# TensorE reads a run-time tile's second weights where they stand, by a register that holds the expert

## The chip, the cores and the metric

One core of one Trainium2 chip runs the whole program. The metric is the time of one execution on the device, in microseconds (us). The engines are named as in the profile: PE is TensorE (PEld its weight loads), DVE is VectorE, ACT is ScalarE, POOL is GpSimd and SP is SyncE. A `q` behind a name (PEldq, DVEq, SPq) marks an instruction that the engine's sequencer carries out itself.

## The reference

The first part is a gated recurrence along 4 sequences of 5056 steps with 256 channels. The second part is a layer of 8 experts: each of the 20224 tokens goes to the one expert with the largest gate logit.

```python
f = lower_bound + (1 - lower_bound) * sigmoid(f_logit)
for t in range(S):
    h = f[:, t] * h + (1 - f[:, t]) * x[:, t];  y[:, t] = h      # y: 20224 tokens x 256
logits = y @ w_gate;  e_idx = argmax(logits)                     # 8 experts
gate_w = softmax(logits)[e_idx];  eom = sigmoid(y @ w_output_gate)
for e in range(8):
    mask = e_idx == e
    h = max(y[mask] @ w1[e], 0)                                  # 256 -> 1024
    out[mask] = gate_w[mask] * eom[mask, e] * (h @ w2[e])        # 1024 -> 256
```

## The kernel before

Every float32 matrix product is made of three f16 products: both operands are split into a high and a low f16 half (hh and hl for the hidden layer, the index 0 and 1 in the weights), and high by high, high by low and low by high are added in PSUM.

**Work.** The tokens pass in 40 chunks of 512 (`chunk`, lines 254 to 439). A chunk is loaded, scanned (DVE, L280), split into halves (ACT L310, DVE L314), transposed to rows by SP's DMA (L307), multiplied with the gates on PE (L329), counted by expert on PE (L386), and its rows are scattered by POOL into a scratch memory in DRAM, sorted by expert (L433). At the same time the weights of all experts are scaled and split into `w1s` and `w2s`, which then stay in SBUF for good: `w2s` has for each expert 8 slices, each with a high and a low part of 256 columns.

**Tiles.** Once enough tokens of an expert have come, a plan (`plan`, L476 to L556) on DVE writes a table `pl_tab` with one row a tile: the place of its tokens and its expert. Which expert a tile has is known only at run time. A full tile has two blocks of 128 tokens (nb = 2); after the last chunk what is left of each expert is taken in tiles of one block (nb = 1). In the traced run 82 such run-time tiles were worked, 64 full ones and 18 of one block. Ahead of them, in the first 185 us, come tiles whose expert is fixed in the program (`first1`, `first2`), which read `w1s` and `w2s` where they stand; they are not touched here.

**A run-time tile.** `gather` fetches its tokens by SP's DMA. `expert` (L640) makes DVE's sequencer read the expert from the table into a register. `fetch1` (L654) and `fetch2` (L660) have DVE copy the expert's halves of `w1s` and `w2s`, 128x2048 f16 each, two of either a tile, into the fixed buffers `w1_0`, `w1_1`, `w2_0`, `w2_1`, of which there is one each. `gemm1` (L666) multiplies tokens with the first weights, 12 matmuls for each of four quarters q, ACT makes hh from PSUM (L680) and DVE makes hl (`low`, L688). `gemm2` (L693) multiplies hh and hl, which are loaded as stationary operands, with the second weights, which stream: 6 matmuls of 256 columns for each block and quarter, 48 for a full tile and 24 for one of one block. ACT scales the result (`evacuate`), POOL scatters it (`put`).

**Order.** `experts` (L925 to L963) writes the order by hand: in iteration t, quarter q, PE gets `gemm1` of tile t and then `gemm2` of tile t - 1. The DVE tasks of the quarter (`low`, `fetch1`, `fetch2`, `factors`) are mixed with those of the chunks in flight by `together`, and each engine keeps the order that results (`ordered`). `beside` puts the chunks' small matmuls (L329, L386) one at a time behind groups of three matmuls of `gemm1` and `gemm2`. `fetch2(T, 0)` stands in quarter 3 of tile T's own iteration and `fetch2(U, 1)` in quarter 1 of the next one, always ahead of the `gemm2` that needs it.

Of the kernel before, what the change touches and what calls it, by code (L numbers as in the profile page):

```python
# [9 lines left out]
F16 = mybir.dt.float16  # L10
# [6 lines left out]
ds = bass.ds  # L17
# [4 lines left out]
SMALL, BIG = 1, 2  # L22
# [28 lines left out]
def tile_scan_moe(  # L51
# [10 lines left out]
    nc = tc.nc  # L62
    P = 128
    D, N = xT.shape
    KD = D // P
    E = wgT.shape[2] // 2
    WE = wT.shape[2]
    NF = WE // (2 * D)
# [9 lines left out]
    WH = WE // 2  # L78
    QH = WH // 2
# [4 lines left out]
    def sure(tokens):  # L84
# [19 lines left out]
        out=tri, in_=ones, compare_op=ALU.is_gt, fill=0.0, base=0, pattern=[[1, P]], channel_multiplier=-1  # L104
# [63 lines left out]
    def alone(g):  # L168

        while True:  # L170
            try:
                next(g)
            except StopIteration as end:
                return end.value
# [6 lines left out]
        out=gsq, in0=wgf, scalar=1.0, in1=wgf, op0=ALU.mult, op1=ALU.mult, accum_out=gss  # L181
# [9 lines left out]
        out=wgs[:, :, 1, :], in0=wgc, scalar=gsc, in1=wgs[:, :, 0, :], op0=ALU.mult, op1=ALU.subtract  # L191
# [13 lines left out]
    w2f = w2s.rearrange("p e f h m -> p (e f h m)")  # L205
# [26 lines left out]
    def beside(n=None):  # L232
        for _ in range(len(queue) if n is None else min(n, len(queue))):
            f, a = queue.pop(0)
            f(*a)
# [386 lines left out]
    mpool = {}  # L622
# [17 lines left out]
    def expert(T):  # L640
        yield BIG
        T["ev"] = nc.vector.value_load(T["tab"][T["j"] : T["j"] + 1, 1:2], min_val=0, max_val=E - 1)

    def factors(T):
        nb, ev = T["nb"], T["ev"]
        col = cinv[:, ev : ev + 1] if isinstance(ev, int) else cinv[:, ds(ev, 1)]
        fac = sp.tile([P, 2], F32, tag="fac", name="fac", bufs=4)
        yield SMALL
        nc.vector.tensor_scalar(
            fac[:, 0:nb].unsqueeze(2), T["mt"][:, 0:nb, 0:2].bitcast(F32), col, None, ALU.mult  # L650
        )
        T["fac"] = fac

    def fetch1(T, h):  # L654
        w = mpool["m"].tile([P, QH * 2], F16, tag=f"w1_{h}", name=f"w1_{h}", bufs=1)
        yield BIG
        nc.vector.tensor_copy(out=w, in_=w1f[:, ds(T["ev"] * (2 * WH) + h * 2 * QH, 2 * QH)])  # L657
        T[f"w1_{h}"] = w.rearrange("p (f k h m) -> p f k h m", f=NF // 2, k=KD, h=2)

    def fetch2(T, h):  # L660
        w = mpool["m"].tile([P, QH * 2], F16, tag=f"w2_{h}", name=f"w2_{h}", bufs=1)
        yield BIG
        nc.vector.tensor_copy(out=w, in_=w2f[:, ds(T["ev"] * (2 * WH) + h * 2 * QH, 2 * QH)])  # L663
        T[f"w2_{h}"] = w.rearrange("p (f h m) -> p f h m", f=NF // 2, h=2)

    def gemm1(T, q):  # L666
        mp, n = mpool["m"], T["nb"] * P
        ph = pp.tile([P, 2, 256], F32, tag="h", name="ph", bufs=4)
        w = T[f"w1_{q // 2}"]
        for i in range(2):  # L670
            f = (2 * q + i) % 4
            for k in range(KD):
                first, last = k == 0, k == KD - 1
                o = ph[:, i, 0:n]
                nc.tensor.matmul(out=o, lhsT=w[:, f, k, 0, :], rhs=T["xh"][:, k, 0:n], start=first, stop=False)  # L675
                nc.tensor.matmul(out=o, lhsT=w[:, f, k, 0, :], rhs=T["xl"][:, k, 0:n], start=False, stop=False)  # L676
                nc.tensor.matmul(out=o, lhsT=w[:, f, k, 1, :], rhs=T["xh"][:, k, 0:n], start=False, stop=last)  # L677
                beside(1)
        hh = mp.tile([P, 2, 256], F16, tag="hh", name="hh", bufs=6)
        nc.scalar.activation(hh[:, :, 0:n], ph[:, :, 0:n], AF.Relu)  # L680
        T[f"h{q}"] = (ph, hh)

    def low(T, q):
        n = T["nb"] * P
        ph, hh = T[f"h{q}"]
        hl = mpool["m"].tile([P, 2, 256], F16, tag="hl", name="hl", bufs=6)
        yield BIG
        nc.vector.scalar_tensor_tensor(  # L688
            out=hl[:, :, 0:n], in0=ph[:, :, 0:n], scalar=0.0, in1=hh[:, :, 0:n], op0=ALU.max, op1=ALU.subtract
        )  # L690
        T[f"h{q}"] = (hh, hl)

    def gemm2(T, q):  # L693
        nb = T["nb"]
        if q == 0:
            T["y"] = pp.tile([P, 2, D], F32, tag="y", name="py", bufs=2)
        y, w = T["y"], T[f"w2_{q // 2}"]
        hh, hl = T.pop(f"h{q}")
        for i in range(2):
            f = (2 * q + i) % 4  # L700
            for b in range(nb):
                first = q == 0 and i == 0 and b == 0
                last = q == 3 and i == 1
                c = slice(b * P, (b + 1) * P)
                o = y[:, b, :]
                nc.tensor.matmul(out=o, lhsT=hh[:, i, c], rhs=w[:, f, 0, :], start=first, stop=False, skip_group_check=True)  # L706
                nc.tensor.matmul(out=o, lhsT=hh[:, i, c], rhs=w[:, f, 1, :], start=False, stop=False, skip_group_check=True)  # L707
                nc.tensor.matmul(out=o, lhsT=hl[:, i, c], rhs=w[:, f, 0, :], start=False, stop=last, skip_group_check=True)  # L708
                beside(1)


# [31 lines left out]
    def evacuate(T):  # L743
        nb = T["nb"]
        if isinstance(T["ev"], int):
            T["yo"] = yo = ep.tile([P, 1, D], F32, tag="ey", name="ey", bufs=2)
        else:
            T["yo"] = yo = mpool["m"].tile([P, 2, D], F32, tag="yo", name="yo", bufs=2)
        for b in range(nb):
            nc.scalar.activation(yo[:, b, :], T["y"][:, b, :], AF.Copy, scale=T["fac"][:, b : b + 1])  # L750

    def put(T):
        for b in range(T["nb"]):
            ins = nc.gpsimd.indirect_dma_start(  # L754
                out=out[:, :], out_offset=IOA(ap=T["mt"][:, b, 2:4].bitcast(I32), axis=0), in_=T["yo"][:, b, :],
                in_offset=None, bounds_check=N - 1, oob_is_err=False,
            )
            apart(ins, "out")
# [51 lines left out]
    def step(k, tasks, need=PLAN):  # L810
        prog["left"] += k
        if prog["left"] < 1.0:
            together(tasks)
        while prog["left"] >= 1.0:
            prog["left"] -= 1.0
            pump(tasks, need)
            tasks = []
# [3 lines left out]
    def ahead(t):  # L821
        while len(slots) <= t and len(slots) < ntile:
            plans(1)
            if planning:
                alone(planning.pop(0))
            else:
                pump([], 1)
        while prog["got"] <= t and prog["got"] < ntile:
            tiles[prog["got"]] = gather(prog["got"], slots[prog["got"]])
            prog["got"] += 1  # L830
# [52 lines left out]
    for j in range(-2, nh):  # L883
        tasks = []
# [4 lines left out]
        for z in range(2):  # L889
# [8 lines left out]
            tasks = []  # L898
# [26 lines left out]
    def experts(t0, t1, more):  # L925
        ahead(t0)
        alone(expert(tiles[t0]))
        alone(fetch1(tiles[t0], 0))
        for t in range(t0, t1 + 2):
            T = tiles.get(t) if t < t1 else None  # L930
            U = tiles.get(t - 1) if t0 < t <= t1 else None
            V = tiles.get(t - 2) if t > t0 + 1 else None
            rate = RATE * (T or U or V)["nb"] / 2
            for q in range(4):
                tasks = []
                if q == 0:
                    if t + 1 < t1 + min(more, 1):
                        ahead(t + 1)
                    if T:
                        tasks.append(fetch1(T, 1))  # L940
                elif q == 1:
                    if U:
                        tasks.append(fetch2(U, 1))
                elif q == 2:
                    if t + 1 < t1:
                        alone(expert(tiles[t + 1]))
                        tasks.append(fetch1(tiles[t + 1], 0))
                elif T:
                    tasks.append(fetch2(T, 0))
                    tasks.append(factors(T))  # L950
                if q == 0 and U:
                    tasks.append(low(U, 3))
                if q and T:
                    tasks.append(low(T, q - 1))
                step(rate, tasks)
                if q == 0 and V:
                    evacuate(V)
                if q == 1 and V:
                    put(V)
                if T:  # L960
                    gemm1(T, q)
                if U:
                    gemm2(U, q)  # L963
# [51 lines left out]
```

## Time and profile before

| | |
|---|---|
| time, median of 3 runs | 1020.92 us (1020.44 to 1021.68) |
| the profiled execution's own time | 1019.5 us |
| its span | 1017.8 us |
| PE busy | 917.6 us, 9775 matmuls |
| PEld busy | 822.5 us |
| DVE busy | 886.5 us, of which the copies of L663 111.9 us and of L657 114.9 us |
| ACT / POOL busy | 511.8 / 378.2 us |
| mean granted clock of TensorE | 0.989 |

Busy time is that of the engine alone, without its sequencer. The end of a matmul is modelled in the trace, so that matmuls that follow each other closely overlap in it: how fast PE runs is seen from the distance between the starts of matmuls, not from the length of one. L675 to L677 are `gemm1`'s matmuls, L706 to L708 `gemm2`'s.

### The profile page before, as it was taken

Reading aid. Unit: us, or ns where it says so; the run is one execution under the profiler, and the core shown is the slowest. Engines: PE = TensorE matmul, PEld = TensorE weight load, DVE = VectorE, ACT = ScalarE, POOL = GpSimd, SP = SyncE. Lnnn points to the kernel's source line nnn. Section 1 sums busy time; section 2 is a strip of 40 time slices with the busy share of each in tenths; the row PEclk is TensorE's granted clock in tenths of the full one; section 3 lists DMA queues with packets and bytes.
Section 4 is the critical chain, followed back from the end, with each engine's and each line's share of the span. In section 5 each row is a group of like instructions: output and inputs, shape, how many; then the busy total and the mean of one; then the engine's idle time right before and its main releaser. Section 6 shows DMA issues by size and latency. Waiting matters only on the chain. (4 is left out here: it accounts for less than half of the span.)

```text
span 1017.8 us, 27499 instructions
## 1 busy us (share of the span) xinstructions
PE 917.6 (90%) x9775; PEld 822.5 (81%) x9775; DVE 886.5 (87%) x2803; ACT 511.8 (50%) x1075; POOL 378.2 (37%) x378
## 2 busy tenths in 40 slices
PE   2267998899999999999999999999999999999993
PEld 2156987788888888888888888888888888899993
DVE  7889897899999999999999999999999998758771
ACT  5667684554554555545545455455455543333331
POOL 1532334334344443433444434344444344221121
PEclk9999999999999999999999999999999999999997
DMA  8899976755655556456566555565565644321120
GB/s 311 200 305 271 254 179 147 163 154 137 139 136 151 145 136 163 135 136 142 132 141 156 157 147 133 136 139 132 142 154 135 151 91 97 97 54 43 43 55 16
DMA packets 238546, 146.34 MB, mean 144 GB/s; under 512 B 202557, under 2 KB 204223, under 8 KB 238400
## 3 DMA queue, kind: packets, MB, share of 16 engines
q1 hardware_dynamic: 222752, 101.74, 43.5%
q0 software_dynamic: 15360, 42.74, 13.3%
q8 instruction: 80, 1.31, 0.6%
q14 instruction: 66, 0.54, 0.2%
q10 hardware_dynamic: 288, 0.02, 0.0%
HBM read 58.38 MB, written 44.49 MB: 101 GB/s over the span
## 5 line engine op out<-in xcount | busy, mean ns | idle before, releaser
L675 PE MATMUL ph<-xq,w 128*128 128x256 f16 (+1 forms) x1312 | 331.0, 261 | 3.2 <-DMA xq<-scr 2.7
L677 PE MATMUL ph<-xq,w 128*128 128x256 f16 (+1 forms) x1312 | 331.6, 261 | 0.0
L676 PE MATMUL ph<-xq,w 128*128 128x256 f16 (+1 forms) x1312 | 331.3, 261 | 0.0
L706 PE MATMUL py<-w,hh 128*128 128x256 f16 x1168 | 318.0, 272 | 10.4 <-DVE w L663 5.5
L708 PE MATMUL py<-w,hl 128*128 128x256 f16 x1168 | 318.3, 273 | 0.0
L707 PE MATMUL py<-w,hh 128*128 128x256 f16 x1168 | 318.2, 272 | 0.0
L754 POOL DMA_INDIRECT out_dram<-yo,mt x146 | 165.9, 1137 | 298.4 <-ACT yo L750 270.5
L433 POOL DMA_INDIRECT scr<-rows,dst x154 | 178.9, 1162 | 225.3 <-issue 212.5
L680 ACT ACTIVATE hh<-ph 128x512 f16<-128x512 f32 (+1 forms) x328 | 178.7, 545 | 156.9 <-PE ph L677 154.9
L688 DVE SCALAR_TENSOR_TENSOR hl<-ph,hh 128x512 f16<-128x512 f32 (+1 forms) x328 | 204.8, 625 | 10.4 <-ACT hh L680 8.6
L675 PEld LDWEIGHTS <-w 128*128 128x128 f16 x1312 | 128.0, 98 | 16.5 <-DVE xt L269 3.0
L677 PEld LDWEIGHTS <-w 128*128 128x128 f16 x1312 | 128.1, 98 | 12.1
L657 DVE COPY w<-w1s 128x2048 f16 x164 | 114.9, 701 | 26.2 <-PE ph L677 24.7
L676 PEld LDWEIGHTS <-w 128*128 128x128 f16 x1312 | 127.9, 97 | 9.7
L707 PEld LDWEIGHTS <-hh 128*128 128x128 f16 x1168 | 113.9, 98 | 23.2 <-issue 12.7
L708 PEld LDWEIGHTS <-hl 128*128 128x128 f16 x1168 | 113.9, 98 | 13.5
L706 PEld LDWEIGHTS <-hh 128*128 128x128 f16 x1168 | 113.9, 98 | 11.2
L663 DVE COPY w<-w2s 128x2048 f16 x164 | 111.9, 682 | 0.5 <-PE py L708 0.3
L274 ACT ACTIVATE ft<-ft,fb,fa 128x512 f32<-128x512 f32 (+1 forms) x76 | 60.6, 807 | 97.9 <-DVE xt L269 90.1
L310 ACT ACTIVATE ft<-xt,sa 128x512 f16<-128x512 f32 (+1 forms) x76 | 50.2, 708 | 104.9 <-DVE li L299 100.7
L280 DVE TENSOR_TENSOR_SCAN xt<-ft,xt 128x512 f32<-128x512 f32 (+4 forms) x78 | 90.9, 1173 | 0.0
L750 ACT ACTIVATE yo<-py,fac 128x256 f32<-128x256 f32 x146 | 61.5, 465 | 26.4 <-PE py L708 22.8
(172 smaller groups left out, 1355.0 us busy)
## 6 DMA issues: line engine op xcount, KB each, us to landing
ft<-in_fT_dram SPq DMA_DIRECT2D x37, 512.0 KB
xt<-in_xT_dram SPq DMA_DIRECT2D x37, 512.0 KB
w<-in_wT_dram SPq DMA_DIRECT2D x32, 512.0 KB
scr<-rows,dst POOLq DMA_INDIRECT x154, 2.8
rows<-ft SPq DMA_TRANSPOSE x152
out_dram<-yo,mt POOLq DMA_INDIRECT x146, 2.4
xq<-scr SPq DMA_TRANSPOSE x99
scr<-padt SPq DMA_DIRECT2D x9, 136.0 KB
```

Source lines behind the costliest of these rows:

```text
L433: ins = nc.gpsimd.indirect_dma_start(out=scr[:, :], out_offset=IOA(ap=dst[:, b : b + 1], axis=0), in_=rows[:, b, :], in_offset=None)
L657: nc.vector.tensor_copy(out=w, in_=w1f[:, ds(T["ev"] * (2 * WH) + h * 2 * QH, 2 * QH)])
L663: nc.vector.tensor_copy(out=w, in_=w2f[:, ds(T["ev"] * (2 * WH) + h * 2 * QH, 2 * QH)])
L675: nc.tensor.matmul(out=o, lhsT=w[:, f, k, 0, :], rhs=T["xh"][:, k, 0:n], start=first, stop=False)
L676: nc.tensor.matmul(out=o, lhsT=w[:, f, k, 0, :], rhs=T["xl"][:, k, 0:n], start=False, stop=False)
L677: nc.tensor.matmul(out=o, lhsT=w[:, f, k, 1, :], rhs=T["xh"][:, k, 0:n], start=False, stop=last)
L680: nc.scalar.activation(hh[:, :, 0:n], ph[:, :, 0:n], AF.Relu)
L688: nc.vector.scalar_tensor_tensor(out=hl[:, :, 0:n], in0=ph[:, :, 0:n], scalar=0.0, in1=hh[:, :, 0:n], op0=ALU.max, op1=ALU.subtract)
L706: nc.tensor.matmul(out=o, lhsT=hh[:, i, c], rhs=w[:, f, 0, :], start=first, stop=False, skip_group_check=True)
L707: nc.tensor.matmul(out=o, lhsT=hh[:, i, c], rhs=w[:, f, 1, :], start=False, stop=False, skip_group_check=True)
L708: nc.tensor.matmul(out=o, lhsT=hl[:, i, c], rhs=w[:, f, 0, :], start=False, stop=last, skip_group_check=True)
L754: ins = nc.gpsimd.indirect_dma_start(out=out[:, :], out_offset=IOA(ap=T["mt"][:, b, 2:4].bitcast(I32), axis=0), in_=T["yo"][:, b, :], in_o ...
```

## The change

`fetch2` is gone, and with it two DVE copies of 128x2048 for each run-time tile and the buffers `w2_0` and `w2_1`. Instead PE's own sequencer reads the tile's expert from `pl_tab` into a register, once a tile, at the head of `gemm2`'s first quarter (L691 of the changed kernel). Each of `gemm2`'s matmuls then takes its streaming operand straight out of `w2s`, at an address that is worked out from that register. `gemm1` and its copies (`fetch1`) stay as they were, as do the number, shapes and order of all matmuls.

```diff
-    def fetch2(T, h):
-        w = mpool["m"].tile([P, QH * 2], F16, tag=f"w2_{h}", name=f"w2_{h}", bufs=1)
-        yield BIG
-        nc.vector.tensor_copy(out=w, in_=w2f[:, ds(T["ev"] * (2 * WH) + h * 2 * QH, 2 * QH)])
-        T[f"w2_{h}"] = w.rearrange("p (f h m) -> p f h m", f=NF // 2, h=2)
-
     def gemm1(T, q):
...
         nb = T["nb"]
         if q == 0:
             T["y"] = pp.tile([P, 2, D], F32, tag="y", name="py", bufs=2)
-        y, w = T["y"], T[f"w2_{q // 2}"]
+            T["pv"] = nc.tensor.value_load(T["tab"][T["j"] : T["j"] + 1, 1:2], min_val=0, max_val=E - 1)
+        y = T["y"]
         hh, hl = T.pop(f"h{q}")
         for i in range(2):
-            f = (2 * q + i) % 4
+            at = T["pv"] * (2 * WH) + (2 * q + i) * (2 * D)
+            wh, wl = w2f[:, ds(at, D)], w2f[:, ds(at + D, D)]
             for b in range(nb):
...
-                nc.tensor.matmul(out=o, lhsT=hh[:, i, c], rhs=w[:, f, 0, :], start=first, stop=False, skip_group_check=True)
-                nc.tensor.matmul(out=o, lhsT=hh[:, i, c], rhs=w[:, f, 1, :], start=False, stop=False, skip_group_check=True)
-                nc.tensor.matmul(out=o, lhsT=hl[:, i, c], rhs=w[:, f, 0, :], start=False, stop=last, skip_group_check=True)
+                nc.tensor.matmul(out=o, lhsT=hh[:, i, c], rhs=wh, start=first, stop=False, skip_group_check=True)
+                nc.tensor.matmul(out=o, lhsT=hh[:, i, c], rhs=wl, start=False, stop=False, skip_group_check=True)
+                nc.tensor.matmul(out=o, lhsT=hl[:, i, c], rhs=wh, start=False, stop=last, skip_group_check=True)
...
-                elif q == 1:
-                    if U:
-                        tasks.append(fetch2(U, 1))
...
-                elif T:
-                    tasks.append(fetch2(T, 0))
+                elif q == 3 and T:
                     tasks.append(factors(T))
```

In the changed kernel `gemm1`'s matmuls stand on lines 669 to 671, `low` on 682 and `gemm2`'s matmuls on 702 to 704.

PE's instructions at the start of a full tile's `gemm2`, before the change. The three groups are the first block's high by high, high by low and low by high product; `w_0` is the copied buffer:

```order
L329 MATMUL pr<-wgs,ft 128x16
L706 LDWEIGHTS hh
L706 MATMUL py<-w_0_9416,hh 128x256
L707 LDWEIGHTS hh
L707 MATMUL py<-w_0_9416,hh 128x256
L708 LDWEIGHTS hl
L708 MATMUL py<-w_0_9416,hl 128x256
```

The same place in the changed kernel:

```order
L329 MATMUL pr<-wgs,ft 128x16
L691 TENSOR_LOAD pl_tab
L691 ISA x2
L702 LDWEIGHTS hh
L702 ISA
L702 MATMUL py<-w2s,hh 128x256
L703 LDWEIGHTS hh
L703 ISA
L703 MATMUL py<-w2s,hh 128x256
L704 LDWEIGHTS hl
L704 ISA
L704 MATMUL py<-w2s,hl 128x256
```

Three instructions for the sequencer stand ahead of the tile's first matmul (the load of the register and two that check its value), and one `ISA` stands between every weight load and its matmul: a fused group of three or four register operations, (expert x 4096 + place) x 2 + base, worked out anew for each matmul. The rest of PE's list, and the lists of ACT, POOL and SP, are the same in both kernels.

DVE's instructions in a quarter 2 and the quarters behind it, while a chunk is split into halves (L314), before the change. `w_0` and `w_1` are the buffers of the copies:

```order
L642 TENSOR_LOAD pl_tab
L642 ISA x2
L314 SCALAR_TENSOR_TENSOR ft<-xt,sa,ft 128x512
L657 ISA
L657 COPY w_0_8934<-w1s 128x2048
L688 SCALAR_TENSOR_TENSOR hl<-ph,hh 128x512
L314 SCALAR_TENSOR_TENSOR ft<-xt,sa,ft 128x512
L649 ISA
L649 TENSOR_SCALAR fac<-mt,cinv 128x2
L269 SCALAR_TENSOR_TENSOR xt<-ft,xt 128x512
L663 ISA
L663 COPY w_0_8969<-w2s 128x2048
```

The same place in the changed kernel:

```order
L642 TENSOR_LOAD pl_tab
L642 ISA x2
L314 SCALAR_TENSOR_TENSOR ft<-xt,sa,ft 128x512
L657 ISA
L657 COPY w_0_6310<-w1s 128x2048
L682 SCALAR_TENSOR_TENSOR hl<-ph,hh 128x512
L314 SCALAR_TENSOR_TENSOR ft<-xt,sa,ft 128x512
L649 ISA
L649 TENSOR_SCALAR fac<-mt,cinv 128x2
L269 SCALAR_TENSOR_TENSOR xt<-ft,xt 128x512
L682 SCALAR_TENSOR_TENSOR hl<-ph,hh 128x512
L269 SCALAR_TENSOR_TENSOR xt<-ft,xt 128x512
```

The copy out of `w2s` and its register operations are gone; what stood behind them has moved up. `fetch1`'s copies stay, as does DVE's own load of the expert (L642), which they need.

## The prediction

> **What bounds the kernel now.** I read the page first, then the table by stretches, then the rows of single lines, the waits of the middle stretch, and last the timeline of one chunk.
>
> ```profile
> PE 917.6 (90%) x9775; PEld 822.5 (81%) x9775; DVE 886.5 (87%) x2803; ACT 511.8 (50%) x1075; POOL 378.2 (37%) x378
> ```
>
> PE and DVE are both near full on average. The table by stretches (busy time and count of each engine, granted clock, DMA) parts the span at the first full tile, at the last chunk, and at the tiles of one block:
>
> ```profile
> core 0: us, PE busy (x) PEld busy (x) DVE busy (x) ACT busy (x) POOL busy (x), PEclk, DMA share, GB/s
> 0.00:185.00 185.00, 122.35 (x1652) 111.88 (x1652) 154.96 (x548) 119.18 (x216) 61.73 (x78) 0.98 0.89 234
> 204.00:835.00 631.00, 613.46 (x6025) 543.64 (x6023) 588.15 (x1880) 323.59 (x700) 267.54 (x252) 1.00 0.57 141
> 835.00:906.00 71.00, 71.00 (x683) 63.86 (x681) 53.75 (x177) 23.24 (x49) 21.35 (x21) 1.00 0.34 83
> 912.00:991.00 79.00, 79.00 (x1078) 74.97 (x1077) 62.73 (x136) 29.71 (x74) 16.20 (x15) 1.00 0.22 47
> ```
>
> From 835 us on PE never rests. In the middle stretch it is idle for 17.5 us and DVE is at 93%. The first stretch has no run-time tile, so the change cannot touch it. PE's sequencer has one wait a run-time tile just ahead of `gemm1`, which marks the tiles (last two numbers: start of the first and the last one), for the middle and for the tiles of one block:
>
> ```profile
> L675 PEldq EVENT_SEMAPHORE  x57: 51/51/51, 204.1 to 834.9; - x57
> ```
> ```profile
> L675 PEldq EVENT_SEMAPHORE  x16: 51/51/51, 912.0 to 991.5; - x16
> ```
>
> That is 630.8 / 56 = 11.26 us a full tile and 79.5 / 15 = 5.30 us a tile of one block. What the array itself needs is read from starts in PE's timeline (start, length, line):
>
> ```profile
> 505.48 0.27 PE L675 MATMUL ph<-xq,w 128*128 128x256 f16 x1
> ...
> 508.10 0.27 PE L675 MATMUL ph<-xq,w 128*128 128x256 f16 x1
> ...
> 508.42 0.20 PE L329 MATMUL pr<-wgs,ft 128*128 128x32 f16 x2
> 508.48 0.27 PE L675 MATMUL ph<-xq,w 128*128 128x256 f16 x1
> ```
>
> Between the first two starts lie 12 matmuls of `gemm1` and 12 of `gemm2`: 2.62 / 24 = 0.109 us each. Two gate matmuls take 0.06 us, 0.03 each with its load. A full tile needs 96 x 0.109 = 10.46 us, and half a chunk's 23 small matmuls (16 gates, 5 counts, 2 sums) 0.35: 10.81. So in the middle 0.45 us a tile, 25 us over 56 tiles, is waiting. Where:
>
> ```profile
> 508.80 0.17 PE L329 MATMUL pr<-wgs,ft 128*128 128x16 f16 x1
> 509.23 0.18 PE L329 MATMUL pr<-wgs,ft 128*128 128x16 f16 x1 [0.25 <-DVE ft L314]
> ...
> 509.97 0.20 PE L329 MATMUL pr<-wgs,ft 128*128 128x16 f16 x2
> 510.56 0.27 PE L706 MATMUL py<-w,hh 128*128 128x256 f16 x1 [0.39 <-issue]
> ```
> ```profile
> 508.42 0.75 DVE L314 SCALAR_TENSOR_TENSOR ft<-xt,sa,ft 128x512 f16<-128x512 f32 x1
> ...
> 509.82 0.68 DVE L663 COPY w<-w2s 128x2048 f16 x1
> ```
>
> Two stalls stand close together. At 508.80 PE is held for 0.43 - 0.03 = 0.40 us by DVE's L314. At 509.97 it is held for 0.59 - 0.06 = 0.53 us; the row says "issue", but the copy of L663 ends at 509.82 + 0.68 = 510.50, just ahead of the restart, so it is `fetch2` that PE waits for. The waits of the middle stretch count them:
>
> ```profile
> PE pr L329 <- DVE ft L314: 6.3, 26, 0.4
> PE py L706 <- DVE w L663: 5.5, 14, 0.4
> PE py L706 <- issue: 4.3, 11, 0.4
> ```
>
> About 26 of each, once a chunk: 26 x (0.40 + 0.53) = 24.2 us, nearly all of the 25. (The view gives less for each since the modelled end of a matmul lies 0.16 us behind the start of the next.) The kernel is bound by the array at 0.109 us a matmul, and by a DVE that is late once a chunk.
>
> **What the change removes.**
>
> ```profile
> L663 DVE COPY w<-w2s 128x2048 f16 x164 | 111.9, 682 | 0.5 <-PE py L708 0.3
> ```
>
> 164 copies of 0.68 us leave DVE. By itself that is worth nothing, since DVE is not what most of the time waits for; it is worth what PE waited. The 0.53 us stall was the wait for such a copy: it goes, 26 x 0.53 = 13.8 us. The one at L314 is lateness: DVE runs without a pause into it, four copies of a chunk are 4 x 0.6 = 2.4 us (it starts the next instruction 0.6 us behind a copy's start), and what is lacking is 0.40 us. It should go too, 26 x 0.40 = 10.4 us. Next late are the two chunk sums on PE, which wait for ACT; they are in the last us of the 25 and stay.
>
> **What it adds.** No engine work, but work for PE's sequencer: one register load a tile, and a group of register operations ahead of each matmul of `gemm2`. No trace of before shows either on PE. The nearest rows are DVE's, the same operations for the same addresses (min/median/max in ns):
>
> ```profile
> L642 DVEq TENSOR_LOAD <-pl_tab x82: 298/303/557, 183.6 to 988.8; - x82
> L642 DVEq FUSED_REGOPS  x82: 190/190/213, 184.3 to 989.2; - x82
> L642 DVEq SEQ_ASSERT  x82: 23/23/35, 184.5 to 989.5; - x82
> ```
> ```profile
> L663 DVEq FUSED_REGOPS  x164: 65/70/75, 192.6 to 998.1; - x164
> ...
> L663 DVEq EVENT_SEMAPHORE  x41: 21/21/21, 878.8 to 998.2; - x41
> ```
>
> The head of a tile costs 0.30 + 0.19 + 0.02, with 0.03 between each about 0.61 us. Behind it are queued only that tile's `gemm2` and what follows on PE; the table was written long before, since SP read it to fetch the tile. For one matmul, call the sequencer's whole time X. The group is 65 ns with three operations and 75 with four, and nearly all have four. PE's own simple wait takes 51 ns where DVE's takes 21, so I add 30. Load and matmul add 0.03, as for the gates. X = 75 + 30 + 30 = 0.135 us. Does a register in a matmul's address cost more? On DVE it does not show:
>
> ```profile
> L657 DVEq FUSED_REGOPS  x2: 65/70/75, 506.6 to 507.3; - x2
> ```
> ```profile
> L649 DVEq FUSED_REGOPS  x1: 53/53/53, 506.8 to 506.8; - x1
> ```
>
> Between these two, 506.6 to 506.8, DVE's sequencer did the group and handed over three instructions, one of them a copy with a register address: (200 - 65) / 3 = 45 ns for each at most. The bounds of X are 0.095 (65 + 30) and 0.25 (190, the longest group on any row here, + 60); I take 0.135, from the rows of the same operation.
>
> [...]
>
> X is longer than 0.109, so `gemm2` alone would starve the array. What hides it is `gemm1`, 12 plain matmuls that the sequencer hands over in 12 x 0.03 = 0.36 us while the array takes 1.31, and the distance that it runs ahead. In one tile:
>
> ```profile
> L675 PEldq EVENT_SEMAPHORE x1: 51/51/51, 495.5 to 495.5; - x1
> ```
> ```profile
> 497.49 0.27 PE L675 MATMUL ph<-xq,w 128*128 128x256 f16 x1
> ```
>
> The wait and the matmul right behind it in the list lie 1.9 us apart. A quarter's `gemm2` uses up 12 x (0.135 - 0.109) = 0.31 us of that, the head of a tile 0.61. The sequencer's sum for a full tile is 48 X + 48 x 0.03 + 0.35 + 0.05 + 0.61 = 48 X + 2.45: 8.9 us against the array's 10.81. It keeps up as long as X is under 0.174; if that cover is gone, each 0.01 us of X costs 0.48 us a tile. In a tile of one block `gemm1` has 48 matmuls of 128 columns and `gemm2` 24: the sequencer needs 24 X + 2.1 = 5.34 us against 5.30, 0.04 x 18 = 0.7 us, so about 1.
>
> [...]
>
> **Sum.** -13.8 - 10.4 + 1 = -23.2, of which I leave 1.2 for stalls that don't go wholly: -22. Against the profiled execution, 1019.5 us (span 1017.8): 997.5. The median of the runs is 1.4 us above that execution: 999.
>
> **The rivals.** [...]
>
> Second, about the same: the copy's stall goes, the other stays because L314 is held by what comes before it (ACT's halves and SP's transposes) and not by copies, and X is 0.165. Then -13.8, and in the tiles of one block 6.06 - 5.30 = 0.76 x 18 = +14: 1021. Against it: DVE's 93%.
>
> **How the numbers follow.** The forecast has 0.60: from 994 (nothing is left of the 25 us and the head is hidden) to 1011 (X = 0.165, -24 + 14). The slower rival has 0.30, half of it below 1100. The second has 0.10, mostly within 0.2% (2 us, about what a measurement of this kernel can tell from no change). Faster 0.63, same 0.07, slower 0.30. The range goes from 993 to 1100; what lies above has about 0.15, below it 0.03.
>
> **What would show it.** In the profile of the changed kernel: DVE's busy time down by about 112 us; no wait of `gemm2`'s first line (L702); the register groups' row on PE, with its length; waits of L669 in the middle 10.85 us apart instead of 11.26, and 5.3 in the tiles of one block. I am wrong if these lie 12 and 6.9 us apart, with matmuls of `gemm2` that start 0.2 us apart and no releaser; and half right if L329 still waits for L314.

## The result and the profile after

| | before | after |
|---|---|---|
| time, median | 1020.68 us (1020.25 to 1021.68, 4 runs) | 990.01 us (988.36 to 993.38, 4 runs) |
| the profiled execution, its span | 1019.5, 1017.8 us | 990.77, 989.1 us |

The ratio is 0.9702, with a 95% interval of 0.9675 to 0.973: 3% faster. The forecast of 999 had the direction right and was 9 us too high; 990.0 lies 3 us below the range.

The page of the changed kernel, engines:

```profile
span 989.1 us, 30907 instructions
PE 907.7 (92%) x9775; PEld 819.7 (83%) x9775; DVE 801.0 (81%) x2639; ACT 519.7 (53%) x1075; POOL 390.1 (39%) x378
```

DVE has 164 instructions fewer (2639 instead of 2803). Its busy time fell by 886.5 - 801.0 = 85.5 us, not by the 111.9 us that the copies' own lengths add up to: in the record a copy of 0.68 us overlaps what follows it, which starts 0.60 us behind the copy's start (median), and with each copy 85.5 / 164 = 0.52 us of busy time went away. The table by stretches, for the middle and for the tiles of one block:

```profile
core 0: us, PE busy (x) PEld busy (x) DVE busy (x) ACT busy (x) POOL busy (x), PEclk, DMA share, GB/s
204.00:810.00 606.00, 606.00 (x6052) 543.52 (x6051) 536.85 (x1783) 332.90 (x706) 283.66 (x253) 1.00 0.61 147
882.00:962.00 80.00, 80.00 (x1091) 75.92 (x1089) 45.92 (x107) 30.17 (x76) 15.41 (x16) 1.00 0.23 50
```

PE never rests in the middle any more, and DVE is at 89% instead of 93%. The waits that mark the tiles (L669 is what L675 was), for the middle and for the tiles of one block:

```profile
L669 PEldq EVENT_SEMAPHORE  x57: 51/51/51, 203.6 to 806.8; - x57
```
```profile
L669 PEldq EVENT_SEMAPHORE  x16: 51/51/51, 883.6 to 963.1; - x16
```

A full tile takes 603.2 / 56 = 10.77 us instead of 11.26, and a tile of one block 79.5 / 15 = 5.30 us as before. So the 28.7 us between the two profiled executions' spans lie almost all in one place: (11.264 - 10.771) x 56 = 27.6 us in the middle, 0.5 us ahead of it (204.1 against 203.6), and 0.6 us behind it (1017.8 - 834.9 = 182.9 against 989.1 - 806.8 = 182.3).

The view of waits has no row at all for PE between 196 and 970 us. Who waits now, from the same view over all engines:

```profile
ACT hh L674 <- PE ph L671: 297.4, 257, 2.1
...
DVE hl L682 <- ACT hh L674: 55.4, 91, 2.1
DVE w L657 <- PE ph L671: 33.3, 65, 1.3
...
DVE ft L314 <- ACT ft L265: 18.3, 27, 1.0
```

DVE and ACT wait for PE (first number: us in all, then how often). In the kernel before, PE had waits of its own there, which the prediction shows: 26 for L314 and 25 at L706. Also in the middle, ACT waited for DVE's scans (L280), and DVE for a transfer:

```profile
ACT ft L287 <- DVE xt L280: 36.9, 28, 1.5
...
DVE ft L314 <- DMA rows<-ft: 12.8, 20, 0.6
```

Both rows are gone in the changed kernel. The second shows that of the 7% of the middle in which DVE was not busy (631 - 588 = 43 us), 12.8 us were put down to the transposes at L314. DVE's pause at L314 itself has stayed: the last row of the view of after has it once a chunk, put down to ACT.

What was added, on PE's sequencer: the groups of register operations ahead of `gemm2`'s matmuls, and the head of a tile (min/median/max in ns).

```profile
L702 PEldq FUSED_REGOPS  x1168: 51/55/60, 193.8 to 972.1; - x195
```
```profile
L691 PEldq TENSOR_LOAD <-pl_tab x82: 297/301/637, 192.8 to 968.4; - x82
L691 PEldq FUSED_REGOPS  x82: 151/151/165, 193.5 to 968.8; - x82
L691 PEldq SEQ_ASSERT  x82: 18/18/24, 193.7 to 969.0; - x82
```

For one tile's head, the load (the second of the two, at 963.6) and the first group behind it:

```profile
L691 PEldq TENSOR_LOAD <-pl_tab x2: 303/304/306, 958.3 to 963.6; - x2
```
```profile
L702 PEldq FUSED_REGOPS  x1: 51/51/51, 964.3 to 964.3; - x1
```

That is 0.70 us for a head.

### The profile page after: what moved, and what is told of

It is laid out like the page before. It is cut to its first block, busy times and chain, and to the rows that moved or that the text cites. A ratio compares the mean times of both kernels' runs of the same rounds, so it can differ in the third digit from the quotient of the medians.

```text
span 989.1 us, 30907 instructions
## 1 busy us (share of the span) xinstructions
PE 907.7 (92%) x9775; PEld 819.7 (83%) x9775; DVE 801.0 (81%) x2639; ACT 519.7 (53%) x1075; POOL 390.1 (39%) x378
## 5 line engine op out<-in xcount | busy, mean ns | idle before, releaser
L669 PE MATMUL ph<-xq,w 128*128 128x256 f16 (+1 forms) x1312 | 330.4, 260 | 2.9 <-DMA xq<-scr 2.4
L750 POOL DMA_INDIRECT out_dram<-yo,mt x146 | 175.3, 1201 | 363.2 <-ACT yo L746 339.9
L704 PE MATMUL py<-w2s,hl 128*128 x1168 | 318.5, 273 | 0.0
L703 PE MATMUL py<-w2s,hh 128*128 x1168 | 318.4, 273 | 0.0
L702 PE MATMUL py<-w2s,hh 128*128 x1168 | 318.1, 272 | 0.0
L433 POOL DMA_INDIRECT scr<-rows,dst x154 | 175.7, 1141 | 122.6 <-issue 109.3
L657 DVE COPY w<-w1s 128x2048 f16 x164 | 120.3, 734 | 35.1 <-PE ph L671 33.3
L669 PEld LDWEIGHTS <-w 128*128 128x128 f16 x1312 | 127.9, 98 | 14.3 <-DVE fac L649 2.7
L704 PEld LDWEIGHTS <-hl 128*128 128x128 f16 x1168 | 114.1, 98 | 13.8
L280 DVE TENSOR_TENSOR_SCAN xt<-ft,xt 128x512 f32<-128x512 f32 (+4 forms) x78 | 90.8, 1172 | 0.0
L314 DVE SCALAR_TENSOR_TENSOR ft<-xt,sa,ft 128x512 f16<-128x512 f32 (+1 forms) x76 | 56.2, 744 | 20.1 <-ACT ft L265 18.3
L329 PEld LDWEIGHTS <-ft 128*128 128x128 f16 x600 | 51.7, 99 | 15.1 <-ACT ft L310 4.9
```

Of the source, the lines that this page charges most:

```text
L280: nc.vector.tensor_tensor_scan(out=xt[:, k, a:z], data0=ft[:, k, a:z], data1=xt[:, k, a:z], initial=init, op0=ALU.mult, op1=ALU.add)
L433: ins = nc.gpsimd.indirect_dma_start(out=scr[:, :], out_offset=IOA(ap=dst[:, b : b + 1], axis=0), in_=rows[:, b, :], in_offset=None)
L702: nc.tensor.matmul(out=o, lhsT=hh[:, i, c], rhs=wh, start=first, stop=False, skip_group_check=True)
L703: nc.tensor.matmul(out=o, lhsT=hh[:, i, c], rhs=wl, start=False, stop=False, skip_group_check=True)
L704: nc.tensor.matmul(out=o, lhsT=hl[:, i, c], rhs=wh, start=False, stop=last, skip_group_check=True)
L750: ins = nc.gpsimd.indirect_dma_start(out=out[:, :], out_offset=IOA(ap=T["mt"][:, b, 2:4].bitcast(I32), axis=0), in_=T["yo"][:, b, :], in_o ...
```

## The experiments

Two theories could explain the gain. **Two places**: PE waited once a chunk at each of two places, for a copy and for L314, and each wait belongs to what stands there (the prediction's sum). **Load**: DVE as a whole needed longer for a chunk (two full tiles, 22.5 us, its own pauses included) than PE (21.54 us), and PE paid the difference at whatever it took from DVE last. The rivals on PE's sequencer were tested as well: that its new work costs time, or would with a little more of it.

The three groups of four runs were made on three chips. On the first the kernel before took 1018.8 us (median), on the second 1029.0, on the third 1028.7; ratios are to the kernel before in the same group.

### Both copies back, read by nobody

The changed kernel, with DVE still copying both halves at the old places:

```diff
+    def idle2(T, h):
+        w = mpool["m"].tile([P, QH * 2], F16, tag=f"w2_{h}", name=f"w2_{h}", bufs=1)
+        yield BIG
+        nc.vector.tensor_copy(out=w, in_=w2f[:, ds(T["ev"] * (2 * WH) + h * 2 * QH, 2 * QH)])
...
+                elif q == 1:
+                    if U:
+                        tasks.append(idle2(U, 1))
...
                 elif q == 3 and T:
+                    tasks.append(idle2(T, 0))
                     tasks.append(factors(T))
```

> The changed kernel with both copies of a tile's second weights put back on DVE, at their old places, into buffers that nobody reads; PE still reads w2s by the register. Theory of load (DVE as a whole sets the pace of the middle stage: in the kernel before it worked without a pause at about 22.5 us a chunk, PE needs 21.5): the pace of before comes back though PE waits for no copy, about 1019 us (1014 to 1021), with PE waiting at other lines for DVE. Theory of two places (0.53 us lost at the copy, 0.40 at L314, as predicted): only L314's stall and that of the chunk sums come back, 990 + 13 = about 1003 us. If only the wait for the copied buffer counted: 990 us.

Measured: 1018.31 us, ratio 0.9982 (0.9967 to 0.9998). The whole gain is gone, although no matmul waits for these copies. Tiles in the middle, and PE's waits there:

```profile
L674 PEldq EVENT_SEMAPHORE  x54: 51/51/51, 205.1 to 801.7; - x54
```
```profile
PE pv L291 <- ACT ft L287: 6.2, 21, 0.4
PE pr L329 <- DVE ft L314: 5.5, 24, 0.4
```

And ACT's wait for DVE's scan there, which the changed kernel doesn't have:

```profile
ACT ft L287 <- DVE xt L280: 35.9, 26, 1.5
```

596.6 / 53 = 11.26 us a tile, as before. PE still stands twice a chunk: the wait that was at the copy's reader has moved to the chunk sum L291, which waits for ACT, which waits for DVE. That rules out two places and is what load says. What PE's own new work costs is not seen here, since PE has slack while DVE sets the pace (it is busy for 583.5 us of the 596 between 204 and 800 us); it is seen in the changed kernel, whose array is dense at 10.77 us a tile with all of that work, and in two kernels below, which both take 988 us, one with all of that work (one copy back) and one with half of it (one half by register).

### One copy back, read by nobody

The same with only the copy of the first half (`idle2(T, 0)` in quarter 3).

> The changed kernel with one of the two copies of a tile put back on DVE (the one of quarter 3), unread. Load: DVE then needs 22.5 - 2 x 0.6 = 21.3 us a chunk, less than PE's 21.5, so the time stays at 990 us (988 to 994). Two places: L314 is late again by part of its 0.40 us, 990 to 997 us.

Measured: 988.07 us, ratio 0.9696 (0.9674 to 0.9718): no different from the changed kernel. One copy a tile costs nothing and the next one everything.

```profile
204.00:810.00 606.00, 606.00 (x6053) 543.57 (x6051) 560.02 (x1841) 331.63 (x704) 284.18 (x254) 1.00 0.60 147
```

In this row of the table by stretches DVE is busy for 560.0 us of 606, nearly as long as in the kernel before (564.8 us in the same stretch), and PE is dense all the same. DVE's busy share alone doesn't tell which side of the edge a kernel is on.

### The copies asked for a quarter earlier

The kernel before, with `fetch2(T, 0)` moved to quarter 2 and `fetch2(U, 1)` to quarter 0:

```diff
                         tasks.append(fetch1(T, 1))
-                elif q == 1:
                     if U:
                         tasks.append(fetch2(U, 1))
                 elif q == 2:
+                    if T:
+                        tasks.append(fetch2(T, 0))
...
-                elif T:
-                    tasks.append(fetch2(T, 0))
+                elif q == 3 and T:
                     tasks.append(factors(T))
```

> The kernel before, with both copies of a tile's second weights asked for one quarter earlier, same buffers, same work. Load: DVE has as much to do, so the waiting only moves from the copy to other lines, about 1020 us (1015 to 1025, not faster). Two places: the copy is there in time, its 26 x 0.53 = 14 us go, about 1006 us.

Measured: 1017.73 us, ratio 0.9992 (0.9978 to 1.0007). PE's waits in the middle:

```profile
PE pr L329 <- DVE ft L314: 9.1, 25, 0.4
PE ph L675 <- DVE w L657: 8.2, 26, 0.6
```

The wait for the copy of L663 is gone, as the edit meant; now PE waits for the copy of L657, which the earlier ones have pushed back. A wait removed by order turned up elsewhere at the same price.

### One half by register, the other copied

First the first half by register (quarters 0 and 1), on the kernel before:

```diff
+            if q < 2:
+                at = T["pv"] * (2 * WH) + (2 * q + i) * (2 * D)
+                wh, wl = w2f[:, ds(at, D)], w2f[:, ds(at + D, D)]
+            else:
+                wh, wl = T[f"w2_{q // 2}"][:, f, 0, :], T[f"w2_{q // 2}"][:, f, 1, :]
...
-                elif T:
-                    tasks.append(fetch2(T, 0))
```

> Half of the change: PE reads the first half of a tile's second weights (quarters 0 and 1) by the register, the second half still comes from DVE's copy. Load: 1.2 us a chunk leave DVE, more than the 1 us that PE lost, so the whole gain is there, about 990 us (988 to 995). Two places: the copy's stall goes because nobody waits for it, and L314's mostly too, 990 to 998 us. If each copy had its share of the gain: 1005 us.

Measured: 988.36 us, ratio 0.9697 (0.9683 to 0.9712): half of the change gives all of its gain. Then the other half (`q >= 2` by register, `fetch2(U, 1)` dropped), on the second chip:

> The kernel before with only the second half of w2 read by a register (quarters 2 and 3); the copy of the second half is dropped, that of the first half stays where it was. If VectorE's load a chunk sets the pace: one copy a tile fewer is enough, as when the other half was read by a register, so full tiles 10.77 us apart and 988 us. If each copy holds its own matmuls at its own place: half of the gain, about 1004 us. If it was the first half's copy that hurt, because it is asked for late in the tile: no gain, about 1019 us.

Measured: 1010.78 us, ratio 0.9809 (0.9785 to 0.9832), which looked like a copy's own share. But on this chip PE stood still in the middle with no releaser in the profile, and its granted clock in the first 190 us was 0.84 (the number behind POOL's). The clock alone marks nothing: the three runs with one copy back, with the copies asked for earlier and with the first half by register had 0.89, 0.88 and 0.87 there (0.970, 0.972 and 0.970 over the whole span, against 0.961 here), and two of them took 988 us. A row of the table by stretches, and the longest rows of PE's waits:

```profile
0.00:190.00 190.00, 122.37 (x1562) 111.19 (x1562) 149.21 (x530) 114.23 (x205) 58.62 (x76) 0.84 0.85 223
```
```profile
PE py L712 <- issue: 1.7, 5, 0.4
PE pr L329 <- issue: 1.6, 6, 0.5
```

So it was run again beside the changed kernel itself, on the third chip:

> The changed kernel itself, beside the three runs that follow, on the chip that they run on. In the last runs the kernel before took 1029 us and not 1019, and TensorE stood still for 0.4 to 0.7 us about once a chunk with no releaser in the profile. If that belongs to those runs' chip and not to the kernels: here 0.970 of the kernel before, as first measured.

> Only the second half of w2 read by a register, as before. By VectorE's load: the same as the changed kernel within 0.3%, and no stall of TensorE in the middle. If each copy counts by itself: half way between the changed kernel and the kernel before (0.985 of the latter), as the last runs' 0.981 suggests, with stalls once a chunk.

Measured: the changed kernel 1004.34 us, ratio 0.9762 (0.9736 to 0.9789); the second half alone 1002.18 us, ratio 0.9731 (0.9706 to 0.9755). The two agree within their intervals, so either half is enough, as load says. The "no stall of TensorE in the middle" did not come true: between 225 and 820 us PE waited 3.6 us in all here, and 3.1 us in the changed kernel beside it. The changed kernel's own ratio is 0.6% worse here than at first: part of its gain was not there on this chip (see the end). On the second chip the changed kernel was not run, so how much of the 0.981 there was the chip's stays open.

### Both copies back, a quarter shorter

As the first experiment, with `w[:, 0:1536]` copied instead of all 2048 columns. First on the second chip:

> The changed kernel with both copies back as unread ones, as in the run that took 1018 us, but each copies 1536 columns of 2048. If VectorE's load a chunk sets the pace, the pace is that of 22.5 us a chunk less 4 copies x 0.16 us (a quarter of the copy's 0.68 us, less its fixed part) = 21.86 us, 0.32 us above the array's 21.54: over 28 chunks 9 us above the changed kernel, about 997 us, with full tiles 10.93 us apart. If the number of copies counts (what they wait for, their semaphores, their place in the list) and not their length: 1018 us.

Measured: 1023.52 us, ratio 0.9946 (0.9923 to 0.997). That is between the two theories, on the chip with the unexplained pauses, and decides nothing. Again on the third chip, beside the changed kernel:

> The changed kernel with both copies back, unread, of 1536 columns of 2048. By VectorE's load: 9 us above the changed kernel (0.979 of the kernel before), full tiles 10.93 us apart. If the copies' number counts and not their length: 0.998, as with the unread copies of full length.

Measured: 1013.80 us, ratio 0.9844 (0.982 to 0.9869), 9.5 us above the changed kernel where 9 were expected. (The 0.16 us for a quarter of a copy in the first of the two expectations was the author's estimate. The 0.979 of the second took the changed kernel at 0.970; on this chip it is at 0.976, and 9 us more make 0.985.) Tiles of this kernel and of the changed one on that chip:

```profile
L674 PEldq EVENT_SEMAPHORE  x54: 51/51/51, 233.5 to 819.3; - x54
```
```profile
L669 PEldq EVENT_SEMAPHORE  x56: 51/51/51, 228.8 to 827.5; - x56
```

585.8 / 53 = 11.05 against 598.7 / 55 = 10.89 us, 0.17 us a tile x 57 = 9.6 us. That 9.5 us came so near to the 9 is in part luck, since either median is uncertain by 2 to 3 us and this chip has pauses of its own; but the 0.998 that their number would have given is out of reach. The length of the copies counts, not their number, and with it the time goes through the edge gradually: 0 at one copy a tile, 9.5 us at two of three quarters, some 30 at two.

### Four heads a tile

The changed kernel, with the load of the expert's number at every quarter of `gemm2`. This adds three heads a tile to PE's sequencer and no array work:

```diff
         if q == 0:
             T["y"] = pp.tile([P, 2, D], F32, tag="y", name="py", bufs=2)
-            T["pv"] = nc.tensor.value_load(T["tab"][T["j"] : T["j"] + 1, 1:2], min_val=0, max_val=E - 1)
+        T["pv"] = nc.tensor.value_load(T["tab"][T["j"] : T["j"] + 1, 1:2], min_val=0, max_val=E - 1)
```

> The changed kernel, with the expert's number loaded into a TensorE register at every quarter's gemm2 and not only at the tile's first: three more heads of 0.70 us a run-time tile on TensorE's sequencer, no array work. If the sequencer's sum holds (48 matmuls x 0.133 + 48 x 0.03 + 0.40 + heads), a full tile needs 8.2 + 4 x 0.70 = 11.0 us against the array's 10.77: +0.25 x 57 = 14 us in the middle, +2 behind the last chunk, and in the tiles of one block 7.5 us instead of 5.30, +2.2 x 18 = 39 us: about 1045 us. If the sequencer hides such heads because it runs ahead, at every size of tile: 990 us. If a head also empties the array at once (it can't be hidden at all): 82 x 3 x 0.70 = 172 us more, about 1160 us.

Measured on the second chip: 1036.00 us, ratio 1.0063 (1.0033 to 1.0092). And on the third:

> The changed kernel with the expert's number loaded at each quarter. By the sequencer's sum: 55 us above the changed kernel, full tiles 11.0 us apart, tiles of one block 7.5 us. The last runs gave 1036 us beside 1029 for the kernel before, which is some 38 us above 0.970 of it; if the sequencer gets through the later heads faster than through the first, the tiles of one block lie nearer to 6.5 us apart.

Measured: 1033.02 us, ratio 1.003 (1.0008 to 1.0052), 28.7 us above the changed kernel there, half of the 55 that the sequencer's sum gave. Tiles of one block, of this kernel and of the changed one on the same chip:

```profile
L669 PEldq EVENT_SEMAPHORE  x17: 51/51/51, 900.0 to 1003.6; - x17
```
```profile
L669 PEldq EVENT_SEMAPHORE  x16: 51/51/51, 895.2 to 974.3; - x16
```

103.6 / 16 = 6.48 us against 79.1 / 15 = 5.27, not 7.5. What the sum had wrong is seen where the array is starved, in PE's timeline of this kernel:

```profile
946.08 0.22 PE L671 MATMUL ph<-xq,w 128*128 128x128 f16 x1
946.35 0.27 PE L702 MATMUL py<-w2s,hh 128*128 x1
946.49 0.27 PE L703 MATMUL py<-w2s,hh 128*128 x1
946.62 0.27 PE L704 MATMUL py<-w2s,hl 128*128 x1
946.75 0.27 PE L702 MATMUL py<-w2s,hh 128*128 x1
946.88 0.27 PE L703 MATMUL py<-w2s,hh 128*128 x1
947.02 0.27 PE L704 MATMUL py<-w2s,hl 128*128 x1
```

PE stands after `gemm1`'s last matmul (0.27 us to the next start; in the changed kernel, where it doesn't stand, it is 0.06, from 960.87 to 960.93), and then each register-addressed matmul starts (947.02 - 946.35) / 5 = 0.134 us behind the one before: that is X, seen on the array itself. With it the 6.48 us are 24 x 0.134 + 4 x 0.70 + 48 plain pairs, so a plain load and matmul takes an estimated (6.48 - 3.22 - 2.80) / 48 = 0.010 us of the sequencer, not the 0.03 of the prediction.

The full tiles of this kernel:

```profile
L669 PEldq EVENT_SEMAPHORE  x55: 51/51/51, 232.3 to 826.3; - x55
```

594.0 / 54 = 11.00 us a tile, as expected, against 10.89 in the changed kernel on this chip. With the 1.21 us of a tile of one block that gives 0.11 x 57 + 1.21 x 18 = 28 us, nearly all of the 28.7. But the 11.00 was met by luck: with 0.010 the same sum is 48 x 0.134 + 48 x 0.010 + 0.40 + 2.80 = 10.1 us, less than the array needs. A sum over a tile doesn't show where the sequencer's lead runs out within it. In this trace its wait ahead of `gemm1` lies 0.3 to 1.0 us before the matmul that it belongs to, in the changed kernel's on the same chip 1.3 to 1.65 us. At which matmuls the 0.11 us is lost was not settled.

### The first weights by register too

The change carried on to `gemm1`, with both copies of `fetch1` dropped:

```diff
-        w = T[f"w1_{q // 2}"]
+        if q == 0:
+            T["pv"] = nc.tensor.value_load(T["tab"][T["j"] : T["j"] + 1, 1:2], min_val=0, max_val=E - 1)
         for i in range(2):
-            f = (2 * q + i) % 4
+            f = 2 * q + i
...
+                at = T["pv"] * (2 * WH) + (f * KD + k) * (2 * P)
+                wh, wl = w1f[:, ds(at, P)], w1f[:, ds(at + P, P)]
-                nc.tensor.matmul(out=o, lhsT=w[:, f, k, 0, :], rhs=T["xh"][:, k, 0:n], start=first, stop=False)
+                nc.tensor.matmul(out=o, lhsT=wh, rhs=T["xh"][:, k, 0:n], start=first, stop=False)
```

> The changed kernel carried on to the first weights: gemm1 loads w1 too by the register with the expert, both copies of fetch1 are dropped, and the expert's number is loaded once a tile, ahead of gemm1. DVE loses another 164 copies of 0.70 us. If DVE's load were still what most is worth: no slower than 990 us. If the sequencer's sum holds with 0.133 us for each matmul whose load has a register address: a full tile takes 96 x 0.133 + 1.1 = 13.9 us against 10.77, +3.1 x 57 = 177 us, +24 us behind the last chunk, and a tile of one block 72 x 0.133 + 0.75 = 10.3 us against 5.30, +91 us: about 1280 us. If a load with a register address is dearer than a matmul with one, more than that.

Measured on the second chip: 1719.63 us, ratio 1.6728 (1.6684 to 1.6773). The sign and the mechanism are those of the sequencer's sum; the size is not. The groups at one line of `gemm1`, beside its matmuls, and PE's timeline in this kernel:

```profile
L667 PEldq FUSED_REGOPS  x2624: 2/55/810, 187.8 to 1692.5; - x188
L667 PEld LDWEIGHTS <-w1s x1312: 95/96/152, 187.9 to 1692.4; 128*128 x188
```
```profile
499.92 0.27 PE L666 MATMUL ph<-xq,w1s 128*128 128x256 f16 x1
500.14 0.27 PE L667 MATMUL ph<-xq,w1s 128*128 128x256 f16 x1
500.37 0.27 PE L668 MATMUL ph<-xq,w1s 128*128 128x256 f16 x1
500.60 0.27 PE L666 MATMUL ph<-xq,w1s 128*128 128x256 f16 x1
500.82 0.27 PE L667 MATMUL ph<-xq,w1s 128*128 128x256 f16 x1
```

There are two groups for each load here (2624 for 1312), where `gemm2` has one for each matmul, and 0.90 / 4 = 0.225 us from start to start instead of 0.134. A full tile then needs 48 x 0.225 + 48 x 0.134 + 1.1 = 18.3 us. The middle agrees nearly. The same stretch of this kernel and of the changed one:

```profile
225.00:800.00 575.00, 536.29 (x3193) 296.14 (x3193) 257.18 (x877) 175.22 (x372) 124.15 (x134) 0.98 0.33 84
```
```profile
225.00:800.00 575.00, 575.00 (x5743) 515.72 (x5742) 510.33 (x1687) 316.88 (x668) 272.28 (x242) 1.00 0.62 148
```

3193 matmuls instead of 5743 make it 10.77 x 5743 / 3193 = 19.4 us a tile, with DVE busy for 45% of the time. The last 1.1 us a tile stays unexplained.

## Why the prediction was right in its direction and missed the size

**The bound.** "The kernel is bound by the array at 0.109 us a matmul, and by a DVE that is late once a chunk" holds. The array is now dense at that pace. The size of the loss was read too small. It rested on the array's need, estimated as 10.81 us a tile; the changed kernel shows 10.77, so what could be won was 0.49 us a tile, 27.6 us, and not 25. The term that was too large is the small matmul, which takes (10.77 - 10.46) / 11.5 = 0.027 us and not 0.03. The range's lower end was built on the 25: its 994 is 1019.5 - 25, without the 1.4 us that the forecast adds for the median.

**What goes.** The sum priced the two stalls of a single chunk, 26 x (0.40 + 0.53) = 24.2 us, and the price was right. The distances between the starts of PE's matmuls in the trace of before, over the 56 tiles, exceed those of the changed kernel by 13.8 us where `gemm2` waits for the copy and by 10.1 us at L314. But the two were taken as two things with a reason each, and they were one. "Next late are the two chunk sums on PE, which wait for ACT; they are in the last us of the 25 and stay": this is the step that failed, in its size and in its "stay". In the same distances 2.4 us were lost at the chunk sums and 1.0 at other lines, where the prediction had 0.8 for both: together 27.3 us, nearly all of the 27.6. In the changed kernel 0.1 us of that is left. The chunk sums' wait went with the rest because ACT had been waiting for DVE's scans (36.9 us in 28 waits, none in the changed kernel). With the copies back it even became PE's longest wait (21 times, 6.2 us), and with the copies moved a wait for `fetch1`'s copy took its place (26 times, 8.2 us).

Read as load, the sum is shorter: DVE's list took 22.5 us a chunk, its pauses included, and PE's 21.54. All of the difference goes once DVE is shorter, and for that half of the copies is enough. Nor was 1.2 us to be held back "for stalls that don't go wholly". The lateness was misread in one point: "DVE runs without a pause into it" holds for the 1.9 us ahead of the late L314, but three instructions before it DVE had stood still, in the chunk of the prediction's example for 0.66 us:

```profile
506.55 0.75 DVE L314 SCALAR_TENSOR_TENSOR ft<-xt,sa,ft 128x512 f16<-128x512 f32 x1 [0.66 <-ACT ft L265]
```

DVE pauses there once a chunk, and the pause is a part of the 22.5 us. It stays in the changed kernel and no longer makes PE wait; a kernel without it was not tried. One sign did not come: DVE's busy time fell by 85.5 us and not by about 112, as said above.

**What it adds.** X was forecast at 0.135 and is 0.134. That is luck: the parts were off and made up for each other. The group takes 55 ns and not 105, and the rest, load and matmul included, some 79 and not 30. Since a plain load and matmul takes an estimated 10, a register in the address does cost an estimated 134 - 55 - 10 = some 70 ns more than its group, which the prediction, going by DVE's rows, took as nothing. The 30 ns that it added to DVE's 65 to 75 ns, for PE's wait of 51 ns against DVE's of 21, are not seen in PE's group of 55. The head takes about 0.70 us from the load to the first group, against 0.61: its operations take 0.30 + 0.15 + 0.02 = 0.47 us, and the gaps between them 0.23 and not 0.09. The cover held. In the middle of the changed kernel the sequencer's wait ahead of `gemm1` lies 1.35 to 1.66 us before its matmul, where it was 1.94 in the kernel before.

**The tiles of one block.** A cost of 1 us was expected, since 5.34 us of sequencer stood against 5.30 of array; they stayed at 5.30. The mis-sized term is the 0.03 us for a plain load and matmul, which was an upper end from a place where the array, not the sequencer, set the pace. With the 0.010 us of the four-heads run the sum is 24 x 0.134 + 48 x 0.010 + 0.05 + 0.70 = 4.4 us, and the head is hidden.

**The rivals.** The slower one, in which a register in the address is dear and the sequencer becomes the bound, did not come: X is 0.134 and stayed under the 0.174 up to which, by the prediction's own sum, the sequencer keeps up. An X of about 0.20, on which the range's upper end of 1100 and the sign of matmuls 0.2 us apart stand, was the author's estimate; no run shows it for `gemm2`. That the sequencer can become the bound is real one step further: 1719.6 us with the first weights by register. The one in which L314's stall stays was wrong too, for the same reason as the failed step: it gave the wait to what comes just before L314 (ACT's halves and SP's transposes). DVE does pause for these and still does, but that alone holds nobody once a copy a tile is gone. Its X of 0.165 was too high as well.

**The sum of the miss.** In the profiled execution: 3.4 us in the middle (27.6 - 24.2), 1.2 held back, 1.0 for the tiles of one block, 1.1 ahead of and behind the middle: 6.7, from 997.5 to 990.8. The other 2.2 us are the runs' spread: the median was taken to lie 1.4 us above the profiled execution and now lies 0.8 below it.

## What to carry to other kernels

When an engine that feeds the bound one is late by its whole list, count what it needs for a period against what the bound engine needs, and don't add up the stalls where they happen to show: here taking one away by order moved it (1017.7 us), and taking work away ended all of them, only up to the point where the two are even (988.1 us with one copy a tile left, 990.0 with none). The work that replaced it cost nothing as long as it lay in the slack of the engine that took it over. That was PE's sequencer, with room for one register-addressed operand (48 matmuls of 0.134 us in a tile of 10.77 us) and not for two (another 48 of 0.225 us, 19.4 us a tile).

## What was not expected of the hardware

- A register in the address of a matmul's streaming operand cost one group of 55 ns and 0.134 us in all. In the address of the stationary operand the same form took two groups and 0.225 us.
- Unexpected was also how much the same kernel differs between chips: the kernel before took 1018.8, 1029.0 and 1028.7 us (medians) on three of them, with single runs from 1013.6 to 1023.6 on the first and from 1025.8 to 1032.5 on the other two, and the changed one 990.0 when first measured and 1004.3 on the third. On the slower two, PE paused in the middle, mostly for 0.2 to 0.7 us, with no releaser in the profile. The granted clock doesn't tell the chips apart: in the first 190 us it was 0.84 to 0.96 in the runs on the second, 0.87 to 0.96 on the third and 0.87 to 0.97 on the first (over the whole span of the profiled executions 0.886 to 0.986, 0.968 to 0.987 and 0.970 to 0.987). What the pauses are was not settled, nor why the changed kernel has lost 0.6% of its gain there.
